# A transformer block on one core: exponents of the weights by DMA, weights split in four pieces, four banks for the down product, block pairs two operands at a time

## Chip, cores and metric

One core of a Trainium2 chip runs the whole block in one launch. The metric is the time of one execution on the device in microseconds (us). TensorE multiplies, VectorE and ScalarE do elementwise work and reductions, GpSimd does elementwise work and can issue DMAs, and SyncE (SP) issues most of the DMAs. Each engine works through its own instructions in the order in which the program was built, and waits on semaphores for the others.

## The reference

```python
x = A_x                                     # 1 x 2048 x 576, float32
n = layernorm(x)
q, k, v = split(n @ wqkv)                   # 32 heads of 18
o = softmax(q @ k.T / sqrt(18)) @ v         # per head
h = x + o @ wo
n2 = layernorm(h)
h2 = h + (gelu_tanh(n2 @ w_gate) * (n2 @ w_up)) @ w_down    # 576 -> 4608 -> 576
```

Everything is float32. The kernel splits each float32 operand into a float16 high part and a float16 low part and adds three float16 products (high by high, high by low, low by high).

## The kernel before

The 2048 rows are four blocks of 512 (`NB = 4`, `TB = 512`). The program has four stages.

1. Layer norm and the products for queries, keys and values.
2. Attention: eight groups of four heads by four row blocks, 32 tiles (`n`), each of 16 steps (`kt`). VectorE finds each row's maximum (L533), TensorE the scores (L530, L577), ScalarE the exponentials (L579), TensorE weighs the values (L583). `out_block` (L591 on) divides by the sums; its denominators are written to DRAM and broadcast back (L613, L614).
3. A transition: during the last three tiles and after them, `wo_block` multiplies by `wo` and adds x, `pair_rows` normalizes rows and builds the operands of the next stage, and the first weights are loaded and split.
4. The feed-forward layer. The 4608 columns are 18 chunks of 256, and two chunks make a super-chunk `sc`. Rows are taken in two halves `p`, each of two blocks of 512.

In stage 4 the two row blocks and the two halves of the contraction are combined in Strassen's manner: seven products instead of eight for each matrix. The left operands are sums and differences of the weight's four blocks (`S1` to `S4`, `A12`, `A22`, `A11`, `A21` in `W8`, built on GpSimd at L787 on), the right ones those of the rows (`B22`, `B11`, `B21`, `T1` to `T4`, built by `pair_rows`). `unit(c, p)` makes both matrices' seven products for chunk c and half p: 14 steps, in each one product of seven matmuls (L868) and the elementwise work that follows it: copies and GELUs on ScalarE, adds and gates on VectorE, then the high and the low part of the result (L879, L882). It ends with an add (L939), a gate (L876), a high and a low part. `down(p)` multiplies both chunks' results by `w_down`: 16 steps, in each a group of twelve matmuls into one bank (L279), which VectorE adds to `nat` (L958).

The weights are prepared by generators that are stepped beside this work. `split_chunk(c)` does the gate matrix and then the up matrix of chunk c: `load_matrix` issues ten DMAs into `W8`; five yields pass; `split_matrix` builds the sums, calls `exponents`, and writes high parts (ScalarE, L796), low parts (VectorE, L800) and a fix of the tail rows (L804), first for operands 4 to 6 and then for 0 to 3. `split_down(sc)` loads 512 rows of `w_down` into `df`, which is the same memory as `W8`, and splits them likewise (L843, L844); its scale depends on both chunks' exponents. `exponents` (L117) takes the largest absolute value of a matrix: VectorE reduces each partition (L125, L128), TensorE transposes the 128 results into a bank (L132), VectorE reduces that row (L134), TensorE multiplies it by ones to bring it to all partitions (L139), and VectorE copies it and shifts out the exponent (L141, L143).

Each `yield` marks a point at which another generator may be stepped; `take(it, n)` steps it n times, `run(it)` steps it to its end. What a step issues stands on each engine's queue behind what was issued before it. One turn of the main loop, from the second super-chunk on, issues:

- `run(nxt[0])`, then `unit(c, 0)` with the preparation beside it (called U1 in the prediction)
- `run(nxt[1])`, then `unit(c + 1, 0)` (U2) with `split_down` beside it
- `run(nxt[2])`, `down(0)` (D1), then `unit(c, 1)` (U3) alone
- `unit(c + 1, 1)` (U4) and `down(1)` (D2), with the preparation of the next super-chunk beside them

`nxt` holds the two `split_chunk` and the `split_down` of the next super-chunk. `beside` takes two steps of the preparation at every other step of the main work and one at the others.

Banks: `unit` uses six of the eight 2 KB banks (`banks`: three for the gate, three for the up matrix; the sixth, u[2], is the first half of the tile `pairs2[1]`). `m_ring` gives banks for the maxima and for `wo_block`; in stage 4 it and `down_ring` are the same ring of two banks, `singles[3]` and the second half of `pairs2[1]`.

`pair_rows(p)` works on four row blocks i of 128 rows: VectorE normalizes two rows' halves, GpSimd builds T1 to T4 (L718 on), then in two pieces (four operands, three operands) VectorE makes high and low parts, and SP issues transposing DMAs (L748) into the operands' place in `X` or `V`. It issues four transposes per i. Half 0 is done beside the last attention tile (n = 31, from kt = 9), half 1 beside `down(0)` of the first super-chunk, in both pieces through the same buffer.

## Time and profile before

| | us |
|---|---|
| median of three runs | 2969.67 (2966.55 to 2971.0) |
| the profiled execution | 2965.44 |
| its span in the profile | 2963.7 |
| TensorE, VectorE, ScalarE, GpSimd busy | 2697.1, 2247.1, 1590.2, 524.8 |

How to read the lines in the prediction. A row of a timeline is: start in us from the start of the span, duration in us, engine, line, operation, output<-inputs, shape, type, count of instructions drawn together; a bracket at its end gives idle time of the engine just before and what ended it. PE is TensorE, DVE is VectorE, ACT is ScalarE, POOL is GpSimd, SPq the issuing of DMAs on SP's queue. A row of the windows is: the window, its length, busy us (and instructions) of PE, PE's weight loads, DVE, ACT and POOL, the granted clock of TensorE, the busy share of the DMA engines and GB/s. A row of the groups has busy us in total, mean ns of one, idle time before them and its releaser. The chain of waits lists what the end of the program waited for, in order of time. Line numbers are those of the kernel before. Names of tiles are those of memory regions: `W`, `WK`, `A`, `V` and `X` are large ones that several uses share.

### The profile page before, as it was taken

Reading aid. Unit: us, or ns where it says so; the run is one execution under the profiler, and the core shown is the slowest. Engines: PE = TensorE matmul, PEld = TensorE weight load, DVE = VectorE, ACT = ScalarE, POOL = GpSimd, SP = SyncE. Lnnn points to the kernel's source line nnn. Section 1 sums busy time; section 2 is a strip of 40 time slices with the busy share of each in tenths; the row PEclk is TensorE's granted clock in tenths of the full one; section 3 lists DMA queues with packets and bytes.
Section 4 is the critical chain, followed back from the end, with each engine's and each line's share of the span. In section 5 each row is a group of like instructions: output and inputs, shape, how many; then the busy total and the mean of one; then the engine's idle time right before and its main releaser. Section 6 shows DMA issues by size and latency. Waiting matters only on the chain.

```text
span 2963.7 us, 43958 instructions
## 1 busy us (share of the span) xinstructions
PE 2697.1 (91%) x16755; PEld 1110.7 (37%) x16755; DVE 2247.1 (76%) x4068; ACT 1590.2 (54%) x1826; POOL 524.8 (18%) x683
## 2 busy tenths in 40 slices
PE   7999999999999999999967699999999999999999
PEld 3542222222222222222323345555555555555555
DVE  6369999999999999999775556565656565656563
ACT  4218888888888888888542133333333333333332
POOL 2102421212121211212140211111111111111100
PEclk9999999999999999999988899999999999999999
DMA  7221010101010100100141211010101010101011
GB/s 211 66 68 49 14 36 13 34 14 38 14 37 14 28 18 19 33 16 23 47 96 40 54 42 36 20 36 20 36 20 36 20 36 20 36 20 37 20 50 41
DMA packets 170855, 111.99 MB, mean 38 GB/s; under 512 B 84596, under 2 KB 151924, under 8 KB 170644
## 3 DMA queue, kind: packets, MB, share of 16 engines
q1 hardware_dynamic: 165284, 99.90, 12.4%
q0 software_dynamic: 5360, 9.29, 1.2%
q8 instruction: 131, 2.15, 0.3%
q14 instruction: 80, 0.66, 0.1%
HBM read 74.45 MB, written 14.42 MB: 30 GB/s over the span
## 4 chain that ended last, share of the span: by engine, by line
DVE 55%; PE 35%; ACT 4%; DMA 3%; issue 2%; SPq 1%; POOL 0%; DVEq 0%; ACTq 0%; POOLq 0%
DVE mx L533 39%; PE pair L279 9%; PE bank L279 9%; PE bank L868 8%; PE pair L868 7%; DVE WK L882 2%; DVE ac_m L125 1%; ACT WK L879 1%; DMA A<-in_B_w_down_dram 1%; DVE nat L958 1%; DVE W L844 1%; DVE tmp L876 1%; DVE W L800 1%; PE bank L583 1%; DMA X<-A 1%
## 5 line engine op out<-in xcount | busy, mean ns | idle before, releaser
L533 DVE TENSOR_REDUCE mx<-bank 128x1 f32<-128x512 f32 x2048 | 1264.6, 682 | 25.4 <-PE bank L530 25.3
L579 ACT ACTIVATE WK<-pair,p_ex_sc 128x1024 f32<-128x1024 f32 x1024 | 1084.5, 1113 | 236.7 <-PE pair L577 235.6
L583 PE MATMUL bank<-WK,V 128*32 128x512 f32 x4096 | 548.3, 607 | 0.1
L279 PEld LDWEIGHTS <-WK 128*128 128x128 f16 x3456 | 338.1, 98 | 156.4 <-issue 51.6
L868 PEld LDWEIGHTS <-W 128*128 128x128 f16 (+1 forms) x2394 | 234.2, 98 | 317.0 <-issue 50.0
L530 PE MATMUL bank<-W 54*128 54x512 f16 x1024 | 289.8, 381 | 38.0 <-DVE mx L533 9.4
L530 PE MATMUL bank<-A 54*128 54x512 f16 x1024 | 279.1, 380 | 35.2 <-DVE mx L533 6.5
L279 PE MATMUL bank<-W,WK 128*128 128x288 f16 x1824 | 253.6, 287 | 29.9 <-DVE nat L958 20.3
L279 PE MATMUL pair<-W,WK 128*128 128x288 f16 x1632 | 226.4, 289 | 21.7 <-DVE nat L958 18.3
L583 PEld LDWEIGHTS bank<-WK,V 128*32 128x32 f32 x4096 | 81.2, 108 | 433.3 <-issue 405.3
L868 PE MATMUL pair<-X,W 128*128 128x512 f16 (+1 forms) x792 | 221.6, 384 | 22.2 <-ACT tmp L889 10.3
L868 PE MATMUL pair<-V,W 128*128 128x512 f16 (+1 forms) x720 | 203.1, 380 | 8.5 <-ACT tmp L918 3.0
L606 POOL TENSOR_TENSOR rp<-rc,minus_one 128x16 f32<-128x16 f32 x28 | 81.8, 2923 | 617.3 <-DMA rc<-nat 617.3
L787 POOL TENSOR_TENSOR A<-A 128x384 f32<-128x384 f32 x36 | 36.3, 1007 | 807.6 <-DVE A L804 407.9
L796 ACT ACTIVATE W<-A,p_s_m 128x1152 f16<-128x1152 f32 (+1 forms) x52 | 72.6, 1412 | 198.2 <-DVE p_s_m L171 198.2
L577 PE MATMUL pair<-W 56*128 56x512 f16 x1024 | 158.7, 378 | 6.0 <-ACT WK L579 5.3
L577 PE MATMUL pair<-A 56*128 56x512 f16 x1024 | 156.1, 376 | 1.5 <-ACT WK L579 0.8
L958 DVE SCALAR_TENSOR_TENSOR nat<-bank,p_dsc,nat 128x288 f32<-128x288 f32 x152 | 78.3, 515 | 97.9 <-PE bank L279 95.8
L530 PEld LDWEIGHTS <-W 54*128 54x128 f16 x1024 | 59.0, 93 | 221.1 <-issue 219.3
L530 PEld LDWEIGHTS <-A 54*128 54x128 f16 x1024 | 56.7, 93 | 208.7 <-issue 205.3
L958 DVE SCALAR_TENSOR_TENSOR nat<-pair,p_dsc,nat 128x288 f32<-128x288 f32 x136 | 70.0, 515 | 81.3 <-PE pair L279 80.0
L868 PEld LDWEIGHTS <-A 128*128 128x128 f16 x882 | 86.2, 98 | 108.2 <-DMA X<-A 5.4
(279 smaller groups left out, 2913.2 us busy)
## 6 DMA issues: line engine op xcount, KB each, us to landing
A<-in_B_w_down_dram SPq DMA_DIRECT2D x9, 1152.0 KB
A<-in_B_w_up_dram SPq DMA_DIRECT2D x72, 128.0 KB
A<-in_B_w_gate_dram SPq DMA_DIRECT2D x68, 128.0 KB
nat<-rc SPq DMA_DIRECT2D x32, 256.0 KB
qk_hi<-qk SPq DMA_DIRECT2D x36, 128.0 KB
qk_lo<-qk SPq DMA_DIRECT2D x36, 128.0 KB
A<-in_A_x_dram SPq DMA_DIRECT2D x32, 144.0 KB
out_dram<-nat SPq DMA_DIRECT2D x16, 288.0 KB
```

Source lines behind the costliest of these rows:

```text
L279: nc.tensor.matmul(dst, a, b, start=(i == 0), stop=(i == len(pairs) - 1))
L530: nc.tensor.matmul(pms[j][:, :TB], Q[r, q0 : q0 + P], K[r, kc * TB : (kc + 1) * TB], start=True, stop=True)
L533: nc.vector.tensor_reduce(mx[:, t, 2 * pr + j, kc : kc + 1], pms[j][:, :TB], axis=AX.X, op=ALU.max)
L577: nc.tensor.matmul(pS[:, j, :TB], K[r, kt * P : (kt + 1) * P], Q[r, qc * TB : (qc + 1) * TB], start=True, stop=True)
L579: nc.scalar.activation(pes[(2 * kt + pr) % NPE], pS[:, :, :TB], AF.Exp, scale=ex_sc)
L583: nc.tensor.matmul(acc[32 * hh : 32 * hh + 32, :TB], Vg[n // NB][:, kt * G4 + hh * VC : kt * G4 + hh * VC + 32], pes[(2 * kt + hh // 2) % ...
L606: nc.gpsimd.tensor_tensor(rc, den, minus_one.to_broadcast([P, R]), op=ALU.pow)
L787: nc.gpsimd.tensor_add(W8[:, S1], W8[:, A21], W8[:, A22])
L796: nc.scalar.activation(wh[:, a:b], W8[:, a:b], AF.Copy, scale=s)
L868: nc.tensor.matmul(bank, w, x_, start=start and i == 0, stop=i == len(mm) - 1, skip_group_check=not start)
L882: nc.vector.tensor_sub(hl[:, 2 * i + j], v, hh[:, 2 * i + j])
L958: nc.vector.scalar_tensor_tensor(nat[:, t, ws], pt[:, :HALF], dsc, nat[:, t, ws], op0=ALU.mult, op1=ALU.add)
```

## The change

- `exponents` no longer uses TensorE: the 128 partial maxima (256 for the down matrix) are written to DRAM, read back into all 128 partitions, and reduced there on VectorE. Four yields lie between the issue of the two DMAs and the reduce.
- `split_matrix` writes its seven operands in four pieces (4 and 5, 6, 0 and 1, 2 and 3) with two yields each, and has a yield with the value "ready" ahead of them; `wait` for a load is 7 yields.
- `load_matrix` broadcasts the tail rows with one DMA per block: eight DMAs in place of ten.
- `down_ring` has four banks of its own: the second half of `pairs2[1]`, `singles[3]`, and two of those that `unit` uses.
- `beside` always takes two steps.
- `pair_rows` works in four pieces of two (the last: one) operands, through three buffers for half 0 and two for half 1; the high part of half 1 is made on ScalarE; it issues six transposes per i. Half 1 follows on `split_down(0)` and so begins in `unit(1, 0)`.
- Chunk 1's gate matrix is loaded and its maximum found during attention's end (`second`, up to "ready"), and the first loads go on GpSimd's queue.
- The tail matmul of `product` takes 128 rows in place of 96.

```diff
     nc.gpsimd.memset(neg, -MSC)
+    am_dram = [dram.tile([2 * P], F32, name=f"am{i}") for i in range(2)]
+    rows_used = []
+
     def exponents(views, name):
         n = len(views)
...
                 yield
         nc.vector.tensor_reduce(am, ac, axis=AX.X, op=ALU.max)
         yield
-        pt = next(m_ring)
-        for i in range(n):
-            nc.tensor.transpose(pt[0:1, i * P : (i + 1) * P], am[:, i : i + 1], id32)
-        a1 = small.tile([1, n], F32, tag=f"a1{n}", name=f"a1_{name}")
-        nc.vector.tensor_reduce(a1, pt[0:1, : n * P].rearrange("o (n p) -> o n p", n=n),
-                                axis=AX.X, op=ALU.max)
-        nc.vector.tensor_scalar_max(a1, a1, 2.0 ** -60)
-        yield
-        pb = next(m_ring)
-        nc.tensor.matmul(pb[:, :n], ones[0:1], a1, start=True, stop=True)
+        row = am_dram[len(rows_used) % 2]
+        rows_used.append(name)
+        bc = view(WK, 22016, (n * P,))
+        nc.sync.dma_start(row[: n * P].rearrange("(p n) -> p n", n=n), am)
+        nc.sync.dma_start(bc, row[: n * P].unsqueeze(0).to_broadcast([P, n * P]))
+        for _ in range(4):
+            yield
         ab = small.tile([P, n], F32, tag=f"ab{n}", name=f"ab_{name}")
-        nc.vector.tensor_copy(ab, pb[:, :n])
+        nc.vector.tensor_reduce(ab, bc.rearrange("q (p n) -> q n p", n=n), axis=AX.X, op=ALU.max)
+        nc.vector.tensor_scalar_max(ab, ab, 2.0 ** -60)
         e = small.tile([P, n], I32, tag=f"e_{name}", name=f"e_{name}")
         nc.vector.tensor_scalar(e, ab.bitcast(I32), 23, None, op0=ALU.logical_shift_right)
         yield
...
             return XT[:, k % 9, o : o + TB]
         return VP[:, p * PIECES + k - 18]
-    def pair_rows(p, region, off, parts_of):
+    def pair_rows(p, region, off, parts, high):
         F7 = view(region, off, (7, HALF))
         B22, B11, B21, T1, T2, T3, T4 = (F7[:, i] for i in range(7))
         F1 = F7.rearrange("p a b -> p (a b)")[:, HALF : HALF + D]
-        for rows in parts_of:
-            nc.gpsimd.memset(rows.rearrange("p (a b) -> p a b", b=5 * P)[:, :, 5 * P - KR :], 0.0)
+        C = 5 * P
+        M2, M3 = 2 * P, 3 * P
+        for rows in parts:
+            nc.gpsimd.memset(rows[:, :, M3 - KR : M3], 0.0)
         for i in range(TPB):
             t1, t2 = 2 * p * TPB + i, (2 * p + 1) * TPB + i
             normed(F1, nat[:, t1], t1)
...
             nc.gpsimd.tensor_sub(T3, B22, b12)
             nc.gpsimd.tensor_sub(T4, B21, T2)
             yield
-            for q, (o0, o1) in enumerate(((0, 4), (4, 7))):
+            for q, (o0, o1) in enumerate(((0, 2), (2, 4), (4, 6), (6, 7))):
                 f = F7[:, o0:o1]
-                rows = parts_of[q]
-                n = o1 - o0
-                r = rows[:, : n * 5 * P].rearrange("p (a b) -> p a b", b=5 * P)
-                M2 = 2 * P
-                nc.vector.tensor_copy(r[:, :, :M2], f[:, :, :M2])
-                nc.vector.tensor_copy(r[:, :, 2 * M2 : 2 * M2 + KR], f[:, :, M2:])
+                rows = parts[q % len(parts)]
+                r = rows[:, : o1 - o0]
+                high(r[:, :, :HALF], f)
                 yield
-                nc.vector.tensor_sub(r[:, :, M2 : 2 * M2], f[:, :, :M2], r[:, :, :M2])
-                nc.vector.tensor_sub(r[:, :, 2 * M2 + KR : 2 * M2 + 2 * KR], f[:, :, M2:],
-                                     r[:, :, 2 * M2 : 2 * M2 + KR])
-                nc.gpsimd.tensor_copy(r[:, :, 2 * M2 + 2 * KR : 2 * M2 + 3 * KR],
-                                      r[:, :, 2 * M2 : 2 * M2 + KR])
+                nc.vector.tensor_sub(r[:, :, M3:], f[:, :, :M2], r[:, :, :M2])
+                nc.vector.tensor_sub(r[:, :, HALF : HALF + KR], f[:, :, M2:], r[:, :, M2:HALF])
+                nc.gpsimd.tensor_copy(r[:, :, HALF + KR : HALF + 2 * KR], r[:, :, M2:HALF])
                 k0, k1 = 5 * o0, 5 * o1
+                flat = rows.rearrange("p a b -> p (a b)")
                 for a, b in ((0, 9), (9, 18), (18, 35)):
                     a, b = max(a, k0), min(b, k1)
                     if a >= b:
...
                     else:
                         v = p * PIECES + a - 18
                         dst = VP[:, v : v + b - a, i * P : (i + 1) * P]
-                    nc.sync.dma_start_transpose(dst, rows[:, (a - k0) * P : (b - k0) * P])
+                    nc.sync.dma_start_transpose(dst, flat[:, (a - k0) * P : (b - k0) * P])
                 yield
...
             for a in range(2):
                 eng.dma_start(W8[:, b + a, :2], main[:, a * P : (a + 1) * P].rearrange(
                     "(c p) f -> p c f", p=P))
-            for r in range(3):
-                eng.dma_start(W8[r * KR : (r + 1) * KR, b : b + 2, 2], tail)
+                eng.dma_start(W8[: 3 * KR, b + a, 2], tail[:, a].unsqueeze(0).to_broadcast(
+                    [3, KR, P]))
     def split_matrix(c, m, hi_on=None):
...
         e = yield from exponents([view(A, W8O + 4 * 4 * KT * P, (2, 2 * KT * P))], f"m{m}")
         nc.vector.tensor_copy(ee[:, m, c % 2 : c % 2 + 1], e)
         s = pow2(e, -1, 266, f"s_m{m}")
-        for a, b in ((4, 7), (0, 4)):
+        yield "ready"
+        for a, b in ((4, 6), (6, 7), (0, 2), (2, 4)):
             if hi_on is None:
                 nc.scalar.activation(wh[:, a:b], W8[:, a:b], AF.Copy, scale=s)
             else:
...
             yield
             nc.vector.scalar_tensor_tensor(wl[:, a:b], W8[:, a:b, :2], s, wh[:, a:b, :2],
                                            op0=ALU.mult, op1=ALU.subtract)
-            yield
             r = slice(2 * KR, 3 * KR)
             nc.vector.scalar_tensor_tensor(wh[r, a:b, 2], W8[r, a:b, 2], s[r], wh[r, a:b, 2],
                                            op0=ALU.mult, op1=ALU.subtract)
...
     scales = [None, None]
-    def split_chunk(c, loaded=False, hi_on=None, wait=5):
+    def until_ready(it):
+        for v in it:
+            yield
+            if v == "ready":
+                return
+
+
+    def split_chunk(c, loaded=False, hi_on=None, wait=7, eng=nc.sync):
         for m, src in enumerate((w_gate, w_up)):
             if m or not loaded:
-                load_matrix(src, c)
+                load_matrix(src, c, eng)
                 for _ in range(wait):
                     yield
             yield from split_matrix(c, m, hi_on)
-    def load_down(sc):
-        nc.sync.dma_start(df, w_down[2 * sc * FC : 2 * (sc + 1) * FC, :].rearrange(
+    def load_down(sc, eng):
+        eng.dma_start(df, w_down[2 * sc * FC : 2 * (sc + 1) * FC, :].rearrange(
             "(c p) n -> p c n", p=P))
-    def split_down(sc, wait=5):
-
-        load_down(sc)
+    def split_down(sc, wait=5, eng=nc.sync):
+
+        load_down(sc, eng)
         for _ in range(wait):
             yield
         ed = yield from exponents([df[:, :2], df[:, 2:]], "dn")
...
         return dsc
     banks = [singles[0], singles[1], singles[2], pairs2[0][:, 0], pairs2[0][:, 1], pairs2[1][:, 0]]
+    down_ring = ring([pairs2[1][:, 1], singles[3], singles[1], pairs2[0][:, 1]])
     tmps = []
     tmp_ring = ring(tmps)
...
             ks = [piece(p, 5 * b + k) for k in range(5)]
             mm = []
             for k in range(2):
-                mm += [(wh[:, a, k], ks[k]), (wh[:, a, k], ks[2 + k]), (wl[:, a, k], ks[k])]
-            mm += [(wh[: 3 * KR, a, 2], ks[4][: 3 * KR])]
+                mm += [(wh[:, a, k], ks[k]), (wh[:, a, k], ks[3 + k]), (wl[:, a, k], ks[k])]
+            mm += [(wh[:, a, 2], ks[2])]
             for i, (w, x_) in enumerate(mm):
                 nc.tensor.matmul(bank, w, x_, start=start and i == 0,
                                  stop=i == len(mm) - 1,
...
             for b in range(1, NB):
                 yield from qk_tile(j, b, next(pair_ring)[:, 0])
+    second = split_chunk(1, eng=nc.gpsimd)
     kept = []
     def keep(it):
...
                 fill = wo_block(qc - 1, m_ring)
                 if qc == 2:
                     fill = chain(fill, pair_rows(0, V, 2 * PIECES * TB + 8960, [
-                        view(V, 2 * PIECES * TB + o, (n * 5 * P,), F16)
-                        for o, n in ((0, 4), (4 * 5 * 2 * P, 3))]))
+                        view(V, 2 * PIECES * TB + 2560 * i, (2, 5 * P), F16) for i in range(3)],
+                        nc.vector.tensor_copy))
             if g == 0 and qc == 0 and kt == NT - 1:
                 run(fill)
                 init_set(sets[1])
...
                 blank_rows()
                 load_matrix(w_gate, 0, nc.gpsimd)
             if n == NS - 2 and kt == NT // 2:
-                side = split_chunk(0, True, nc.vector.tensor_scalar_mul)
+                side = chain(split_chunk(0, True, nc.vector.tensor_scalar_mul, eng=nc.gpsimd),
+                             until_ready(second))
     run(side)
     run(fill)
     weigh(*prev)
...
     next(ob)
     tmps += [small.tile([P, TB], F32, tag="tmp", name="tmp", bufs=3) for _ in range(3)]
     tmps += [view(WK, 19968, (TB,)), view(V, 2 * 2 * PIECES * TB, (TB,)), view(W, 33792, (TB,), F32)]
-    down_ring = m_ring = ring([singles[3], pairs2[1][:, 1]])
+    m_ring = ring([singles[3], pairs2[1][:, 1]])
     it = unit(0, 0)
+    side = second
     take(it, 2)
     take(ob)
     take(it, 3)
     take(ob)
+    take(side, 2)
     take(it, 2)
     fill = wo_block(NB - 1, m_ring)
-    side = split_chunk(1)
     for _ in range(2 * TPB):
         take(fill)
         take(side)
...
         take(side, 2)
     run(side)
-    def beside(main, side, every=2):
-
-        for i, _ in enumerate(main):
-            take(side, 1 + (i % every == 0))
-
-    nxt = [iter(()), iter(()), keep(split_down(0))]
-    side = chain(*nxt)
+    def beside(main, side, n=2):
+
+        for _ in main:
+            take(side, n)
+
+    nxt = [iter(()), iter(()), keep(split_down(0, eng=nc.gpsimd))]
+    side = chain(nxt[2], pair_rows(1, A, MAT, [
+        view(A, MAT + 4 * 7 * HALF + 2560 * i, (2, 5 * P), F16) for i in range(2)], nc.scalar.copy))
     for sc in range(NCH // 2):
         c = 2 * sc
         last = sc == NCH // 2 - 1
...
         beside(unit(c + 1, 0), side)
         run(nxt[2])
         dsc = kept.pop()
-        if sc == 0:
-            side = pair_rows(1, A, MAT, [view(A, MAT + 4 * 7 * HALF, (4 * 5 * P,), F16)] * 2)
         beside(down(0, dsc, last), side)
         run(side)
         if sc == 0:
```

## The prediction

> **What bounds the kernel now.** I read the page's span first, then busy time by window, then TensorE's timeline over one period of the last stage. "Product" is seven matmuls of L868, "group" twelve of L279; one super-chunk (two chunks of 256 columns of the feed-forward layer) is a period.
>
> ```profile
> span 2963.7 us, 43958 instructions
> 220.00:1455.00 1235.00, 1161.20 (x7927) 271.54 (x7925) 1223.43 (x2034) 1050.50 (x1019) 280.78 (x405) 1.00 0.10 25
> 1455.00:1743.00 288.00, 206.25 (x1186) 100.01 (x1185) 164.19 (x354) 88.90 (x108) 66.18 (x80) 0.88 0.28 62
> 1743.00:2963.00 1220.00, 1136.56 (x6574) 640.58 (x6571) 732.79 (x1418) 384.47 (x552) 146.40 (x132) 1.00 0.10 31
> ```
>
> The page is of an execution whose span is 2963.7 us. From 220 to 1455 us VectorE is busy 1223 of 1235 us (attention's row maxima): it is the limit there, and the change puts nothing into that stage before its last tiles. From 1743 on TensorE is busy 1137 of 1220 us at full clock, so what remains are its waits. Between lies a transition of 288 us with TensorE busy only 206 us and a clock of 0.88. One period, by the first product or group of each part (TensorE's timeline; the bracket is idle time before and its releaser):
>
> ```profile
> 1878.45 1.68 PE L868 MATMUL bank<-X,W 128*128 128x512 f16 x7
> 1901.24 1.27 PE L279 MATMUL bank<-W,WK 128*128 128x288 f16 x9
> 1931.78 1.68 PE L868 MATMUL bank<-X,A 128*128 128x512 f16 x7
> 1954.23 1.68 PE L868 MATMUL bank<-X,W 128*128 128x512 f16 x7
> 1980.57 1.63 PE L279 MATMUL bank<-W,WK 128*128 128x288 f16 x12
> 2005.47 1.68 PE L868 MATMUL bank<-X,A 128*128 128x512 f16 x7
> 2026.68 1.68 PE L868 MATMUL bank<-X,W 128*128 128x512 f16 x7
> ...
> 1987.83 1.63 PE L279 MATMUL bank<-W,WK 128*128 128x288 f16 x12
> ```
>
> Six parts: the odd chunk's second half U4 (1878.45 to 1901.24), the down product of that half D2 (to 1931.78), the next even chunk's first half U1 (to 1954.23), the odd chunk's U2 (to 1980.57), D1 (to 2005.47), U3 (to 2026.68). U3 has nothing beside it: 21.21 us, which is 14 products of 1.515 without a wait. The twelve last groups of D1 (1987.83 to 2005.47) follow each other after 1.47 us, so a down product without waits is 16 x 1.47 = 23.52. Against these, U4 loses 1.58, D2 7.02, U1 1.24, U2 5.13, D1 1.38 and U3 nothing: 16.35 of the 148.23 us. What the change can give or take in the steady stage is a change of this sum, eight times (the ninth super-chunk has no next one beside its second half). The waits:
>
> ```profile
> 1888.30 0.27 PE L132 MATMUL bank<-id,am_m 128*1 128x128 f32 x1 [0.59 <-DVE am_m L128]
> 1890.64 1.02 PE L868 MATMUL pair<-X,W 128*128 128x512 f16 x4 [0.25 <-DVE ab_m L141]
> 1902.98 0.42 PE L279 MATMUL bank<-W,WK 128*128 128x288 f16 x2 [0.47 <-ACT WK L879]
> 1904.03 0.30 PE L279 MATMUL bank<-W,WK 128*128 128x288 f16 x1 [0.63 <-DVE WK L882]
> 1907.29 1.63 PE L279 MATMUL bank<-W,WK 128*128 128x288 f16 x12 [1.03 <-DVE nat L958]
> 1961.00 2.74 PE L868 MATMUL pair<-X,W 128*128 128x512 f16 x7 [2.06 <-ACT V L889]
> 1963.53 2.34 PE L868 MATMUL bank<-V,W 128*128 128x512 f16 x7
> 1619.12 0.37 PE L132 MATMUL bank<-id,am_m 128*1 128x128 f32 x1 [8.48 <-DVE am_m L128]
> 1620.55 3.14 PE L868 MATMUL bank<-X,W 128*128 128x512 f16 x7
> ```
>
> Maxima through TensorE cost U4 0.59 and 0.25; D2's first group waits for the unit's last ScalarE and VectorE steps (0.47, 0.63), the third for its bank (1.03, since two banks alternate); in U2 a wait of 2.06 for a ScalarE copy is followed by products of 2.74 and 2.34 where 1.68 is normal, 1.72 more. The last two rows are of the transition: 8.48 us for maxima, then a product of 3.14, 1.46 more than normal.
>
> **The change part by part.** *The maxima.* Per matrix two transposes or one, a matmul and two VectorE operations leave; two DMAs on SP's queue and a VectorE reduce of 128 or 256 elements come. The trace has no such trip. Nearest is the softmax's denominators, written to DRAM and broadcast back:
>
> ```profile
> 1562.74 0.33 SPq L613 DMA_DIRECT2D rc<-rc  x1
> 1564.15 0.59 SPq L614 DMA_DIRECT2D nat<-rc  x1
> ...
> 1564.15 4.50 DMA nat<-rc
> ```
>
> The write's completion releases the next issue 1.41 us after its own. The read costs between the 0.59 of its issue and 4.50 (256 KB; here 64 or 128 KB), so the trip is 2.0 to 5.9; I take 4.2, nearer to the upper row because it is the same kind of broadcast. The old way took 2.3 us, from the transpose at 1888.30 to the product at 1890.64 whose matmul stands behind the copied maximum. The change leaves four yields of cover, and two are taken per step: two steps, 3.0 us. So TensorE loses its short waits in U4 and U1, but VectorE, which executes in order, stands 0 to 2.9 us (1.2 by my value) at the reduce, with the unit's adds and gates queued behind it, and ScalarE's GELUs behind these.
>
> *The pace.* A matrix now has 24 yields (7 wait for the load, 8 in the maxima, 1 "ready", 8 in four pieces); before 16. Two chunk matrices are 48, both chunks 96. Two takes per step give 28 in U4, 32 in D2, 28 in U1: 88. The 8 left are precisely the whole split of the odd chunk's up matrix, which the code then flushes between U1 and U2, as the order of built instructions shows: all VectorE and ScalarE pieces stand behind U1's last ones and ahead of U2's first. Before, at 1.5 per step, 64 yields ended inside U1. U2's second product needs that matrix. VectorE's and ScalarE's rows for the pieces and for U1's end are:
>
> ```profile
> 1957.35 0.69 DVE L939 TENSOR_TENSOR W<-pair,W 128x512 f32<-128x512 f32 x1
> 1959.58 0.69 DVE L882 TENSOR_TENSOR WK<-V,WK 128x512 f16<-128x512 f32 x1 [0.68 <-ACT WK L879]
> ...
> L796 ACT ACTIVATE W<-A,p_s_m 128x1536 f16<-128x1536 f32 x26 | 40.8, 1569 | 0.0
> L796 ACT ACTIVATE W<-A,p_s_m 128x1152 f16<-128x1152 f32 x26 | 32.6, 1255 | 198.2 <-DVE p_s_m L171 198.2
> L800 DVE SCALAR_TENSOR_TENSOR W<-A,p_s_m,W 128x1024 f16<-128x1024 f32 x18 | 23.0, 1280 | 6.9 <-ACT W L796 6.8
> L800 DVE SCALAR_TENSOR_TENSOR W<-A,p_s_m,W 128x768 f16<-128x768 f32 x18 | 18.3, 1015 | 13.2 <-ACT W L796 13.2
> L804 DVE SCALAR_TENSOR_TENSOR W<-A,p_s_m,W 32x512 f16<-32x512 f32 x27 | 20.1, 743 | 0.4
> ```
>
> With T the end of U1's last product: add, gate, high and low take 2.9 us (1957.35 to 1960.27), so VectorE is there at T+3.2; reduce and exponents, six short operations of about 0.2, T+4.3. ScalarE's pieces by the slope of its two rows (0.31 us for 384 elements) are 0.94 and 0.63: T+5.9. VectorE's low parts follow (768 and 1024 elements differ by 0.265, so 0.75 and 0.48, with a tail of 0.5 between): T+7.0. TensorE needs it at T+1.5 and can run two of the product's seven matmuls (0.43) earlier: a stall of 5.1 to 5.8, I take 5.3. The slow clock after it costs at least the 1.46 of one slow product and at most 2.9, two of them; I take 2.0, near the 1.72 of the row at 1961.00.
>
> *U2, the down matrix.* Its load waits until the flushed split has read the same region, about T+10. The rows of the old chain:
>
> ```profile
> 1957.39 0.39 SPq L822 DMA_DIRECT2D A<-in_B_w_down_dram  x1
> 1963.08 1.41 DVE L125 TENSOR_REDUCE ac_dn<-A 128x1 f32<-128x576 f32 x2 [2.21 <-DMA A<-in_B_w_down_dram]
> 1971.61 1.44 ACT L843 ACTIVATE W<-A,p_s_dn 128x576 f16<-128x576 f32 x2 [3.60 <-DVE p_s_dn L171]
> ```
>
> The load takes 5.7, the scale is there 14.2 us after the load's issue (1971.61); with a trip of 4.2 for 2.3 that is 16.1: T+26.1. ScalarE stands at the first scaled copy (it stood 3.60 us already), and the copy that frees bank g0 for the eleventh product is behind it: free at T+27.5, a scaled copy and its own 0.7 later. TensorE arrives at T + 10 x 1.515 + 5.3 + 2.0 = T+22.5 to 24. Stall 3.5 to 5.0, I take 4.4, plus a slow clock of 0 to 2.9 (1.4). U2 then loses 5.3+2.0+4.4+1.4 = 13.1 (10.1 to 16.6).
>
> *Down product on four banks.* The bank waits go: D2's rest 7.02-1.10 = 5.92 becomes 0.3 (0 to 1.0), D1 1.3 (1.0 to 1.5). But the ring's first bank is half of the pair that holds the unit's last product, so the first group now waits for the last add of U4.
>
> ```profile
> 1886.25 1.80 DVE L125 TENSOR_REDUCE ac_m<-A 128x1 f32<-128x768 f32 x2
> ```
>
> VectorE in U4 stands until about 13.7 us after its start (load and block sums 7.8 as at 1886.25, reduces 1.8, trip 4.2), then has 4.6 us of pieces and some 7 x 0.7 of unit operations, and 1 to 2 us of waits on ScalarE: the add is done 4 to 5 us after TensorE's last product. Loss at this boundary 4.6 with a clock loss of 1.4, 6.0 (4.5 to 7.9); before, 1.58 and 1.10. U1 0.2 (0 to 0.5).
>
> Sum after: 6.0+0.3+0.2+13.1+1.3 = 20.9, from 15.6 (4.5+0+0+10.1+1.0) to 27.5 (7.9+1.0+0.5+16.6+1.5). Against 16.35 that is +4.6 (-0.8 to +11.2) a period, +37 us (-6 to +89) for eight.
>
> *Transition.* D1 of the first super-chunk carries the rows of block pairs:
>
> ```profile
> 1648.88 1.27 PE L279 MATMUL bank<-W,WK 128*128 128x288 f16 x9
> 1666.41 3.04 PE L279 MATMUL pair<-W,WK 128*128 128x288 f16 x12 [6.75 <-DVE nat L958]
> 1680.68 3.04 PE L279 MATMUL pair<-W,WK 128*128 128x288 f16 x12 [5.84 <-DVE nat L958]
> 1706.33 3.17 PE L868 MATMUL bank<-X,A 128*128 128x512 f16 x7 [5.09 <-DMA X<-A]
> ...
> 1674.52 2.73 SPq L748 DMA_TRANSPOSE X<-A  x2
> ```
>
> It takes 57.4 instead of 23.5 us, a round of 14.3 for each of four row blocks (1666.41 to 1680.68), because one buffer is filled, transposed and filled again, and VectorE's adds wait in the same queue. After: six transposes per round at 1.37 us of SP (2.73 for two) are a floor of 8.2; 14.3 is the ceiling if two buffers hide nothing; I take 11.5. The rounds begin about 7 us before U2 ends (the down split's 20 yields are ten of U2's 14 steps), and the last transposes land some 3 after: 4 x 11.5 - 7 + 3 = 42, and with TensorE's own rest 45: -12 (-28 to -4). The second chunk loaded during attention takes off part of the 8.48 wait for its maxima: -4 (-8.5 to 0). The first half's eight more transposes (8 x 1.37 = 11 of SP, partly under the row maxima) and the last heads' reciprocal behind a VectorE wait: +4 (0 to 15). The first down matrix's longer chain: +3 (0 to 5). Sum -9 (-36.5 to +16). The gpsimd queue for these loads, the shorter tails' DMAs and the 128-row tail matmul I put at nothing: the loads lie ahead of work that is longer, and a matmul's time goes with its columns; uncovered, one load is the 5.7 above.
>
> Total 2965.4 + 37 - 9 = 2993. (2965.44 is the profiled run's time, 1.7 around its span; the median of the runs is 2969.67, 0.14% above.)
>
> **The rivals.** *Faster: the flush stays hidden.* If VectorE arrives at U1's end without a backlog and the trip is 2.0, so that no reduce blocks, U2 keeps 5.13 and the U4 boundary 2.68: 2.68+0.3+0.2+5.13+1.3 = 9.6, -6.75 x 8 - 9 = -63: 2902. For it: VectorE is busy only 733 of 1220 us. Against: its add at U1's end already comes 3 us late (1957.35). *Only one of U2's two stalls:* the down chain waits anyway while TensorE stalls, so 4.4+1.4 less: 15.1 a period, -10 - 9: 2946. For it: the old chain's 14.2 us passed with a wait of only 2.06. Against: it starts only when the flushed split is done. *Slower still, the clock:* each long stall leaves TensorE slow for two products: the upper sum, +89 - 9 = 3045. For it: 1961.00 and 1963.53 after only 2.06 us idle. The Trainium skill (TensorE: Matmul & The Clock Gate, Part 1: The HAM clock gate) says that the clock halves after an idle window of about 3.4 us and returns after as long a busy one; by that rule, three stalls a period would lose 1.7 us each as an estimate, 5.1 where I take 4.8, and 2995. The row at 1961.00 does not wait for so long an idle time. *The change doesn't do what it says:* the rounds of block pairs stay bound by filling (14.3), and the 12 us are not gained: 3005. For it: SP alone needs 8.2 a round; against: the second buffer.
>
> **How the numbers follow.** Forecast 2993 with 0.42 (its own range 2974 to 3015); hidden flush 0.15; one stall 0.17; clock 0.18; transition not shortened 0.08. Two tenths are left out by 2925 to 3055. 0.2% is 6 us, about what a measurement here can tell from no change. Faster: 0.15 and most of the 0.17, 0.29; same 0.06, from the edges of the forecast and the one-stall case; slower 0.65.
>
> **What would show it.** In the period after: a wait before U2's second product of about 5 us, released by VectorE's or ScalarE's split of the up matrix (right), or none (hidden flush); a wait before its eleventh product, with ScalarE standing for the down scale; D2's first group waiting for L946's add, its other groups without waits; U3 still 21.2 us; rounds of 11 to 12 us in the first D1. The forecast is wrong if the period is under 148 us, or if the transition moves by more than 36.

## The result and the profile after

| | before | after |
|---|---|---|
| median, us | 2970.34 (2966.55 to 2972.71) | 3344.78 (3339.8 to 3355.65) |
| span of the profiled execution, us | 2963.7 | 3353.9 |

The ratio is 1.1267 with a 95% interval of 1.1234 to 1.13: slower by 374 us. The forecast was 2993, 28 above the 2965.4 that it started from, with 3055 as its upper end. The sign was right, the size was not. One of the four executions of a kernel below (four banks alone, the pair's half first) was slow, 4068.51 us at a granted clock of 0.588 where the other three had 0.975 to 0.977, and is left out of its median.

The page of the changed kernel: its span, the chain of waits by engine, and the one group that holds most of the answer (line, engine, operation, tile, shapes, count, busy us and mean ns, idle time before and its releaser).

```profile
span 3353.9 us, 43951 instructions
DVE 45%; PE 28%; DMA 19%; ACT 3%; issue 2%; POOL 1%; SPq 1%; DVEq 0%; ACTq 0%; POOLq 0%
L141 DVE TENSOR_REDUCE ab_m<-WK 128x1 f32<-128x128 f32 x36 | 10.3, 285 | 340.3 <-DMA WK<-am 340.3
```

In the chain, DMA has 19%; in that of the kernel before it had 3%:

```profile
DVE 55%; PE 35%; ACT 4%; DMA 3%; issue 2%; SPq 1%; POOL 0%; DVEq 0%; ACTq 0%; POOLq 0%
```

The new reduce L141 is busy 10.3 us in 36 instructions, and VectorE stood idle ahead of them for 340.3 us until the read of the maxima had landed: 9.7 us in each of 35 waits, where the prediction had 1.2.

One period by parts (windows; the columns are those of the windows before: length, busy us of TensorE, weight loads, VectorE, ScalarE and GpSimd, clock, DMA share, GB/s). In order: U3, U4, D2, U1, U2, D1.

```profile
1928.33:1949.48 21.15, 21.15 (x100) 9.56 (x98) 8.12 (x12) 7.82 (x13) 0.00 (x0) 1.00 0.00 1
1949.48:1986.23 36.75, 23.49 (x99) 10.08 (x98) 19.18 (x36) 11.56 (x19) 4.38 (x4) 0.85 0.12 22
1986.23:2016.80 30.57, 26.45 (x192) 19.99 (x192) 17.21 (x36) 3.71 (x5) 2.94 (x4) 0.90 0.13 27
2016.80:2048.57 31.77, 23.09 (x101) 9.97 (x99) 16.36 (x34) 10.08 (x16) 5.23 (x6) 0.84 0.13 29
2048.57:2095.91 47.34, 28.08 (x99) 10.84 (x98) 24.26 (x53) 15.01 (x24) 0.52 (x1) 0.78 0.16 41
2095.91:2119.43 23.52, 23.52 (x192) 18.78 (x192) 9.12 (x17) 0.62 (x1) 4.28 (x4) 1.00 0.01 3
```

| lost, us | U4 | D2 | U1 | U2 | D1 | sum |
|---|---|---|---|---|---|---|
| before | 1.58 | 7.02 | 1.24 | 5.13 | 1.38 | 16.35 |
| forecast | 6.0 (with D2's first wait) | 0.3 | 0.2 | 13.1 | 1.3 | 20.9 |
| after | 15.5 | 7.1 | 10.6 | 26.1 | 0.0 | 59.3 |

U3, which has nothing beside it, takes 21.15 us as before, and D1 is without a wait. The four parts that have a matrix's maxima beside them lost the time, and their clock is 0.78 to 0.90. This period is 42.9 us longer than the one before (191.10 against 148.23), and it is one of the shorter ones: from the first U3 to the last the eight periods take 1549.2 us against 1186.8, 362 more. The transition adds 28, since the first U3 starts at 1734.15 where it started at 1706.33. Together that is the 390 us between the two profiled spans; the profiled execution is the slowest of the four, 11 us above their median. TensorE's timeline shows where the time went:

```profile
1734.15 3.15 PE L875 MATMUL bank<-X,A 128*128 128x512 f16 x7 [5.43 <-DMA X<-A]
1974.69 3.15 PE L875 MATMUL pair<-V,W 128*128 128x512 f16 x7 [8.42 <-ACT tmp L925]
1986.23 2.98 PE L280 MATMUL pair<-W,WK 128*128 128x288 f16 x12 [4.84 <-DVE V L946]
2006.56 3.04 PE L280 MATMUL bank<-W,WK 128*128 128x288 f16 x12 [4.11 <-DVE nat L965]
2033.20 1.01 PE L875 MATMUL pair<-V,W 128*128 128x512 f16 x2 [8.69 <-DVE WK L903]
2061.56 1.03 PE L875 MATMUL pair<-X,W 128*128 128x512 f16 x2 [11.31 <-ACT W L796]
2087.24 2.42 PE L875 MATMUL bank<-V,W 128*128 128x512 f16 x7 [4.54 <-ACT tmp L921]
```

The first row is the transition's end (the last transposes). None of the other releasers is a DMA: they are VectorE's adds, ScalarE's copies and, at 2061.56, a high part of the split (L796), which stood behind something else. What that was is seen on VectorE (timeline, U1), in the chain of waits and on SP's queue:

```profile
2017.07 0.15 DVE L131 TENSOR_REDUCE am_m<-ac_m 128x1 f32<-128x2 f32 x1
2017.14 0.51 DVE L965 SCALAR_TENSOR_TENSOR nat<-pair,p_dsc,nat 128x288 f32<-128x288 f32 x1
2029.07 0.28 DVE L141 TENSOR_REDUCE ab_m<-WK 128x1 f32<-128x128 f32 x1 [11.43 <-DMA WK<-am]
2032.46 0.69 DVE L903 TENSOR_TENSOR WK<-pair,WK 128x512 f32<-128x512 f32 x1
...
2017.57 7.44 DMA am<-am_m
2025.02 4.02 DMA WK<-am
2076.30 3.32 DMA am<-am_dn
2079.63 3.97 DMA WK<-am
...
2017.09 0.37 SPq L778 DMA_DIRECT2D A<-in_B_w_up_dram  x1
2017.57 0.40 SPq L136 DMA_DIRECT2D am<-am_m  x1
2025.02 0.34 SPq L137 DMA_DIRECT2D WK<-am  x1
```

The partial maxima are ready at 2017.22. The write takes 7.44 us and the read 4.02. VectorE reaches the reduce at 2017.64, 0.1 us after the write is issued, and stands 11.43 us. U1's add L903 comes at 2032.46 and TensorE's next product, which needs its bank, at 2033.20 after 8.69 us. The write of the down matrix's maxima, with two values per partition, takes only 3.32. Over the whole chain 36 writes of one value average 7.5 us, six of two values 3.3, and 43 reads 4.3.

### The profile page after: what moved, and what is told of

Read it like the earlier page. It is cut to its first block, busy times and chain, and to the rows that moved or that the text cites. A ratio compares the mean times of both kernels' runs of the same rounds, so it can differ in the third digit from the quotient of the medians.

```text
span 3353.9 us, 43951 instructions
## 1 busy us (share of the span) xinstructions
PE 2774.7 (83%) x16611; PEld 1132.6 (34%) x16611; DVE 2285.6 (68%) x4187; ACT 1612.0 (48%) x1910; POOL 539.1 (16%) x723
## 4 chain that ended last, share of the span: by engine, by line
DVE 45%; PE 28%; DMA 19%; ACT 3%; issue 2%; POOL 1%; SPq 1%; DVEq 0%; ACTq 0%; POOLq 0%
DVE mx L534 34%; DMA am<-am_m 8%; PE pair L280 8%; PE pair L875 7%; PE bank L280 6%; PE bank L875 6%; DMA WK<-am 5%; DMA A<-in_B_w_down_dram 2%; DVE ac_m L128 1%; DMA am<-am_dn 1%; DMA nat<-rc 1%; DVE A L800 1%; PE bank L531 1%; DVE W L800 1%; DMA A<-in_A_x_dram 1%
## 5 line engine op out<-in xcount | busy, mean ns | idle before, releaser
L875 PEld LDWEIGHTS <-W 128*128 128x128 f16 x2394 | 250.3, 105 | 671.8 <-issue 321.6
L280 PEld LDWEIGHTS <-WK 128*128 128x128 f16 x3456 | 353.8, 102 | 207.1 <-issue 101.0
L875 PE MATMUL pair<-V,W 128*128 128x512 f16 x720 | 238.8, 437 | 166.9 <-ACT tmp L925 47.0
L875 PE MATMUL pair<-X,W 128*128 128x512 f16 x792 | 240.3, 401 | 107.4 <-ACT W L796 102.5
L280 PE MATMUL pair<-W,WK 128*128 128x288 f16 x1728 | 243.7, 299 | 48.7 <-DVE tmp L946 28.6
L280 PE MATMUL bank<-W,WK 128*128 128x288 f16 x1728 | 244.2, 301 | 44.7 <-DVE nat L965 44.7
L141 DVE TENSOR_REDUCE ab_m<-WK 128x1 f32<-128x128 f32 x36 | 10.3, 285 | 340.3 <-DMA WK<-am 340.3
L796 ACT ACTIVATE W<-A,p_s_m 128x768 f16<-128x768 f32 x104 | 83.0, 845 | 313.6 <-DVE p_s_m L172 313.6
L875 PE MATMUL bank<-V,W 128*128 128x512 f16 x414 | 117.7, 417 | 46.5 <-ACT tmp L921 16.9
L875 PE MATMUL bank<-X,W 128*128 128x512 f16 x468 | 136.5, 423 | 0.0
```

What stands on the lines that cost most here:

```text
L280: nc.tensor.matmul(dst, a, b, start=(i == 0), stop=(i == len(pairs) - 1))
L796: nc.scalar.activation(wh[:, a:b], W8[:, a:b], AF.Copy, scale=s)
L875: nc.tensor.matmul(bank, w, x_, start=start and i == 0, stop=i == len(mm) - 1, skip_group_check=not start)
```

## The experiments

All kernels compute the whole reference. Times are medians; the kernel before stood at 2966 to 2969 beside them.

**Maxima by TensorE in the changed kernel**, at the same number of yields. The theory T was that the trip is the cost, F that the flush is, O that other parts are.

```diff
-        nc.sync.dma_start(row[: n * P].rearrange("(p n) -> p n", n=n), am)
-        nc.sync.dma_start(bc, row[: n * P].unsqueeze(0).to_broadcast([P, n * P]))
+        pt = next(m_ring)
+        for i in range(n):
+            nc.tensor.transpose(pt[0:1, i * P : (i + 1) * P], am[:, i : i + 1], id32)
...
         for _ in range(4):
             yield
+        pb = next(m_ring)
+        nc.tensor.matmul(pb[:, :n], ones[0:1], a1, start=True, stop=True)
```

> The changed kernel with its maxima spread by TensorE as before (two bank tiles, transpose, matmul), at the same number of yields, so that the flush between U1 and U2 stays. Theory T (the trip through DRAM, 7.4 us to write and 4.2 to read for each matrix where 4.2 in all was forecast, holds VectorE and nearly everything behind it): the waits at the reduce (340 us over 35) go, the time falls by 330 to 400 us to 2945 to 3015. Rival F (the flush and the pace are the cost): the waits before U2's second product stay near 11 us and the time stays above 3200. Rival O (banks, block pairs, queues of the first loads): above 3250, and the steady period stays near 190 us.

Measured 3046.15, ratio 1.0254 (1.0239 to 1.0269). 299 of the 374 us are gone. U2's second product (TensorE's timeline) waits 2.40 us where it waited 11.31:

```profile
1807.99 1.04 PE L878 MATMUL pair<-X,W 128*128 128x512 f16 x2 [2.40 <-ACT W L799]
```

That refutes F and O as the main cost. The time is 31 us over T's range, so that the rest of the change is dearer than T had it.

**The same with one yield**, so that nothing is flushed: the preparation of both chunks then ends inside U1, and none of its steps are left to be issued in one go ahead of U2.

```diff
-        for _ in range(4):
-            yield
+        yield
```

> As the first, with one yield in place of four ahead of the copied maximum: 21 yields a matrix, 84 for both chunks, within the 88 that U4, D2 and U1 take, so nothing is left to flush. T: the flush is worth the 5 to 7 us that the prediction gave it, 8 periods: 40 to 60 us less than the first kernel, 2895 to 2965. F: far more than 100 us less than the first kernel.

Measured 3029.89, ratio 1.0207 (1.019 to 1.0224): 16 us less. From the first U3 to the last the two traces differ by 24.1 us, 3.0 a period; the rest is that the transition is 6.8 us longer here. So the flush, taken together with the three yields of cover that went with it, costs less than the 40 to 60 expected, and less than the 7.3 a period of the prediction. One period's parts (TensorE's timeline: U3, D2, U1, D1, U3 begin):

```profile
1866.13 1.67 PE L877 MATMUL bank<-X,A 128*128 128x512 f16 x7
1914.29 2.99 PE L282 MATMUL pair<-W,WK 128*128 128x288 f16 x12 [3.65 <-DVE V L948]
1942.69 1.67 PE L877 MATMUL bank<-X,A 128*128 128x512 f16 x7
1998.38 1.63 PE L282 MATMUL pair<-W,WK 128*128 128x288 f16 x12 [0.79 <-DVE tmp L948]
2021.89 1.67 PE L877 MATMUL bank<-X,A 128*128 128x512 f16 x7
```

U3 and U4 take 48.16, 5.7 over their 42.4; D2 28.40, 4.9 over; U1 and U2 55.69, 13.3 over; D1 is clean. The sum is 23.9 against 16.35, 7.5 more in this period. The eight together are 56.4 us longer than before, so nearly all of the 60 us that are left are in the steady stage.

**Eight bytes per partition.** Each maximum is written twice, as the down matrix's two values are.

```diff
+            am2 = small.tile([P, 2], F32, tag="am2", name=f"am2_{name}")
+            nc.vector.tensor_copy(am2, am.to_broadcast([P, 2]))
...
-        nc.sync.dma_start(row[: n * P].rearrange("(p n) -> p n", n=n), am)
+        nc.sync.dma_start(row.rearrange("(p n) -> p n", n=2), am2)
```

> The changed kernel with each partition's maximum written twice, eight bytes for four (as the down matrix has them), and 128 KB read back for 64. Theory S (the write is slow because of its four-byte pieces): the write of a gate or up matrix falls from 7.4 to about 3.3 us as the down matrix has it, and the time by up to 4.1 x 36 = 148 us, 3200 to 3260. Rival Q (the write stands behind the 128 KB load piece that SP issues 0.47 us ahead of it): the write stays at 7 us or more and the time at 3330 to 3350.

Measured 3236.36, ratio 1.0897 (1.0875 to 1.0919), 108 us less than the changed kernel; VectorE's idle time at the reduces of gate and up matrices falls by about as much, from 340.3 to 228.4 us. From this kernel's SP queue and chain of waits, and then SP's queue at the changed kernel's last up matrix, which has no load near it, with two lines of the view of DMA in the window 3210 to 3218 (40 slices of 0.2 us):

```profile
2004.88 0.38 SPq L783 DMA_DIRECT2D A<-in_B_w_gate_dram  x1
2005.31 0.73 SPq L785 DMA_DIRECT2D A<-in_B_w_gate_dram  x1
...
2006.36 3.36 DMA am<-am_m
2009.73 4.30 DMA WK<-am
...
2031.96 3.15 DMA am<-am_dn
```

```profile
3197.49 0.73 SPq L780 DMA_DIRECT2D A<-in_B_w_up_dram  x1
3210.03 0.35 SPq L136 DMA_DIRECT2D am<-am_m  x1
3217.75 0.34 SPq L137 DMA_DIRECT2D WK<-am  x1
...
DMA  0000300000000000000000000000000000000000
DMA packets 144, 0.00 MB, mean 0 GB/s; under 512 B 144, under 2 KB 144, under 8 KB 144
```

The write of a gate or up matrix falls to 3.36, although two pieces of the next load are issued just ahead of it. And in the changed kernel that write takes 7.7 us (3210.03 to 3217.75) with nothing issued on that queue for nearly 12 us before. So the queue is not the reason (Q falls) and the pieces are (S). The packets of that last write have all moved by 3211.1, nearly all in the fifth slice; for the remaining 6.7 us, until SP can issue the read, nothing moves. The time lies between the last packet and the completion. The pieces of a write lie side by side in DRAM, so that their spacing grew with their size: these runs can't tell the two apart.

**The kernel before with the trip alone**, at its own pace and order.

```diff
-        pt = next(m_ring)
-        for i in range(n):
-            nc.tensor.transpose(pt[0:1, i * P : (i + 1) * P], am[:, i : i + 1], id32)
...
-        yield
-        pb = next(m_ring)
-        nc.tensor.matmul(pb[:, :n], ones[0:1], a1, start=True, stop=True)
...
+        nc.sync.dma_start(row[: n * P].rearrange("(p n) -> p n", n=n), am)
+        nc.sync.dma_start(bc, row[: n * P].unsqueeze(0).to_broadcast([P, n * P]))
+        yield
```

> The kernel before with nothing changed but the trip through DRAM in place of TensorE, with its one yield of cover and so with the pace and order of before. T: slower by 250 to 420 us, 3220 to 3390, with VectorE's wait at the reduce near 10 us a matrix. F: within 30 us of before, since no split is flushed. O: within 60 us of before.

Measured 3348.13, ratio 1.1273 (1.1251 to 1.1296). One part of the change brings as much as the whole; with one yield of cover it costs 379, in the changed kernel, with four, 299.

**Four banks alone in the kernel before**, in the order of the change and with the shared pair's half last.

```diff
+    down_ring = ring([pairs2[1][:, 1], singles[3], singles[1], pairs2[0][:, 1]])
...
-    down_ring = m_ring = ring([singles[3], pairs2[1][:, 1]])
+    m_ring = ring([singles[3], pairs2[1][:, 1]])
```

> The kernel before with nothing but the change's ring of four banks for the down product. The prediction's view B: its waits for banks go (1.03 in D2, 1.06 in D1, some of D2's rest), but the first bank is half of the pair whose other half holds the unit's last product, so D2's and D1's first group wait for the last add (about 3 us, and a slow clock of 1.4): D2 7.0 to 5 to 8, D1 1.4 to 1 to 4, within 25 us of before, 2945 to 2995. Rival N (the banks are the gain of the change, the pair costs nothing): 2925 or less. Rival W (the banks are what costs the 60 us that stay when the trip is taken out): 3010 or more.

The second kernel differs in one line:

```diff
-    down_ring = ring([pairs2[1][:, 1], singles[3], singles[1], pairs2[0][:, 1]])
+    down_ring = ring([singles[3], singles[1], pairs2[0][:, 1], pairs2[1][:, 1]])
```

> The same four banks with the shared pair's half last in the ring and not first, so that the first three groups take banks that are free early. B: no group waits for the unit's last add, 10 to 45 us less than the kernel before, 2925 to 2960. N and W: no difference to the order of the change, within 5 us of the run with it.

Measured 2986.07 (ratio 1.0064, 1.0046 to 1.0083) and 2971.48 (1.0014, 1.0004 to 1.0023). From TensorE's timelines, the first in D2 of the first kernel, the second in D2 of the second:

```profile
1912.31 3.04 PE L279 MATMUL pair<-W,WK 128*128 128x288 f16 x12 [3.22 <-DVE V L940]
```

```profile
1917.02 0.27 PE L132 MATMUL bank<-id,am_m 128*1 128x128 f32 x1 [2.22 <-DVE am_m L128]
```

With the pair's half first, D2's first group waits 3.22 us for the unit's last add and then runs slowly (3.04 for 1.63), as the prediction's view had it. With it last that wait is gone, but nothing is gained: TensorE waits 2.22 us for a matrix's maxima instead, just behind the place where it had waited 1.03 for a bank. The bank waits were not what set the end. The first kernel came out within the 25 us of view B; the second, expected 10 to 45 us below the kernel before, is a miss.

**Split in two pieces** in the kernel with maxima by TensorE.

```diff
-        for a, b in ((4, 6), (6, 7), (0, 2), (2, 4)):
+        for a, b in ((4, 7), (0, 4)):
...
+            yield
```

> The changed kernel with maxima through TensorE at one yield, and the split in two pieces as before: 19 yields a matrix, 76 for both chunks. View P (the four pieces take VectorE and ScalarE more instructions in the units and cost the U4 and U2 parts their 4 to 5 us more): 15 to 45 us less than 3030. View V (the pace of two takes a step and the first bank cost them, not the pieces): within 10 us of 3030.

Measured 3063.75, ratio 1.0328 (1.031 to 1.0345): 34 us more, not less. Both views fall. In this kernel the four pieces, with the two more yields that they bring, are a gain at two takes a step.

**The transition alone**: block pairs, early second chunk, gpsimd queue and tail as changed; maxima, pieces, pace and banks as before. The "ready" value is given by the last yield of `exponents`.

```diff
-        yield "ready"
...
-        yield
+        yield "ready"
         return e
```

> The change's block pairs, early second chunk, gpsimd queue and wider tail alone: maxima by TensorE, the split in two pieces, 16 yields, 1.5 takes a step and two banks as before. The prediction gave the transition -9 us (-36 to +16): 2929 to 2985, with rounds of 11 to 12 us in the first D1; view O (these parts are part of the 60 us that stay): 2995 to 3020.

Measured 2961.57, ratio 0.9982 (0.9973 to 0.9992): 4.3 us less than before, where the prediction had 9. It is the only version that is clear of noise below the kernel before, and by 0.2% only. The last row in the first D1 and U3 (TensorE):

```profile
1704.12 3.14 PE L876 MATMUL bank<-X,A 128*128 128x512 f16 x7 [14.87 <-DMA X<-A]
```

The groups of D1 hardly wait for the rounds any more (1.85 us for `nat` at most, where they waited 6.75); U3 does, 14.87 us for the last transposes. It starts at 1704.12, 2.2 us earlier than before. D1 itself is 8.3 us shorter (49.10 against 57.45), but it begins 6.1 us later, at 1655.02.

**Two takes a step alone** in the kernel before, and the transition's kernel with two takes and four pieces.

```diff
-    def beside(main, side, every=2):
-
-        for i, _ in enumerate(main):
-            take(side, 1 + (i % every == 0))
+    def beside(main, side, n=2):
+
+        for _ in main:
+            take(side, n)
```

> The kernel before with two steps of the preparation at every step of the main work and nothing else. Open is what makes up the some 40 us that stay with maxima by TensorE and no flush beyond the 19 us of the first bank. View V (the pace: a load has 2.5 steps of cover, 3.8 us, for 3.3 steps, so VectorE's reduces and TensorE's transposes wait for it): 15 to 60 us slower, 2980 to 3025. View P (the four pieces): within 10 us of before.

> The transition's kernel (2961.6) with the four pieces (18 yields a matrix, 72 for both chunks) at two takes a step. V: the pace costs, 2975 to 3025, as much as the kernel before loses with two takes. P: the pieces cost 15 to 45 us and the pace nothing; then the kernel before with two takes stays near 2966 and this one is at 2980 to 3005. If the pieces help, as the run with two pieces at 3064 says, this one is below what V gives.

Measured 3064.32 (1.0333, 1.0317 to 1.0348) and 3086.29 (1.04, 1.0382 to 1.0418). The pace alone costs the kernel before 97 us, more than the 60 that were sought. One period's parts as above:

```profile
1875.30 1.68 PE L868 MATMUL bank<-X,A 128*128 128x512 f16 x7
1927.31 1.71 PE L279 MATMUL bank<-W,WK 128*128 128x288 f16 x12
1960.50 1.68 PE L868 MATMUL bank<-X,A 128*128 128x512 f16 x7
2012.00 1.63 PE L279 MATMUL bank<-W,WK 128*128 128x288 f16 x12
2036.18 1.68 PE L868 MATMUL bank<-X,A 128*128 128x512 f16 x7
```

U3 and U4 lose 9.6, D2 9.7, U1 and U2 9.1, D1 0.7: 29.0, 12.7 more than before (10.9 on the mean of eight), spread over the parts that have the preparation beside them, and with no flush at all. The second kernel is a miss: it is above the 3025 of view V, and 22 us above the kernel with two takes alone, though it has the four pieces that gained 34 us a moment ago. The prices of the parts don't add up from kernel to kernel; why the pieces don't help here was not found.

**Bank order in the kernel with maxima by TensorE, and four banks in the transition's kernel** (the second order above in both).

> The changed kernel with maxima by TensorE at one yield, and the four banks in the order in which the shared pair's half comes last. View B (the first bank costs here what it cost the kernel before): 10 to 25 us less than 3030, 3005 to 3020. Rival: the first group's wait becomes a wait for maxima or for the unit's last low part, within 8 us of 3030.

> The transition's kernel with the four banks, shared half last: could beat both kernels by more. If the bank waits are hidden behind the maxima, as in the kernel before, 2956 to 2970; if they are on the path with the new transition, 2925 to 2950.

Measured 3042.97 (1.0261, 1.0245 to 1.0276) and 2965.97 (0.9999, 0.9989 to 1.0008). In the first, the order costs 13 us instead of saving 10 to 25, and the rival (within 8 us) misses too: what the first bank's wait costs by itself is not added to what the pace costs. In the second four banks gain nothing again.

**Longer wait for a load at two takes**, in two and in four pieces, on the kernel before.

```diff
-    def split_chunk(c, loaded=False, hi_on=None, wait=5):
+    def split_chunk(c, loaded=False, hi_on=None, wait=7):
```

> The kernel before with two takes a step and seven yields for a load in place of five, that is 3.5 steps of cover where the kernel before has 3.3. View L (two takes cost 97 us because the reduces come ahead of their load's landing, and VectorE stands): most of the 97 us is back, 2960 to 2990. Rival D (two takes cost because the preparation's work then lies denser on VectorE and ScalarE in the same steps, whatever the cover): 3030 to 3070.

> The same with the split in four pieces: 20 yields a matrix. L: as the one with two pieces, within 15 us, 2955 to 2990. D: the pieces spread the dense work and gain what they gained between 3064 and 3030, 25 to 45 us under the one with two pieces.

Measured 3099.78 (1.0442, 1.0424 to 1.0459) and 3078.22 (1.0374, 1.0357 to 1.039). More cover for the loads makes it worse by 35 us, so L falls as a whole; the pieces give 22 back, a little less than the 25 to 45 of D, whose 3030 to 3070 for the first is missed as well. What each part loses in us, the mean of eight periods by TensorE's timelines (over 42.42 for two units and 23.52 for a down product):

| | U3, U4 | D2 | U1, U2 | D1 | sum |
|---|---|---|---|---|---|
| before | 2.0 | 7.0 | 6.2 | 1.3 | 16.5 |
| two takes alone | 8.5 | 9.3 | 8.8 | 0.7 | 27.3 |
| and a longer wait | 2.1 | 12.5 | 16.1 | 0.7 | 31.3 |
| transition, two takes, four pieces | 9.3 | 5.5 | 15.7 | 0.7 | 31.2 |
| changed, maxima by TensorE, one yield | 6.1 | 4.9 | 12.6 | 0.0 | 23.5 |

So L is right for U4, where the longer wait takes the loss away, and wrong for the sum: more is lost in D2 and in U1 and U2. In the view of waits (engine, operation, releaser: us in all, times, longest) TensorE's largest one is the first line with two takes alone, the second with the longer wait:

```profile
PE bank L279 <- DVE nat L958: 47.6, 33, 5.2
PE bank L132 <- DVE am_dn L128: 46.2, 8, 7.2
```

The first is of the down product's groups, which wait for a bank; the second is 5.8 us for each down matrix's maxima, whose own wait of five yields was not lengthened in these kernels. So the pace costs, and where it costs changes with the rest of the kernel; how much of it is the down matrix's short cover and how much the density of the work is not settled.

## Why the prediction missed

*The step that failed* is the price of the trip: "I take 4.2, nearer to the upper row because it is the same kind of broadcast", with 2.0 and 5.9 as its ends. It measured 11.8 for a gate or up matrix (7.5 and 4.3) and 7.6 for the down matrix. The read was inside the bounds (the row had 4.50). The write was not: the row of 1.41 us moves 64 bytes per partition, and the changed kernel's 4. The prediction corrected the read for its size, in kilobytes, and took the write as if it cost nothing more to move less. The kernel with the trip alone shows that this one term is worth 379 us in the kernel before, and the changed kernel without it is 299 us faster. The cover was taken too long as well: 3.0 for two steps of TensorE, where the mean was 2.1 (11.8 less the 9.7 of VectorE's wait) and in U1 0.1, since VectorE had nothing else ahead of the reduce.

*What followed from the term.* The mechanism was put rightly: VectorE, in order, stands at the reduce with the unit's adds and gates behind it. With 11.8 in place of 4.2 it stands 9.7 us in the mean and not 1.2, and each of the five matrices of a period passes it on to TensorE, with a slow product behind it (3.15, 3.04). U1, to which 0.2 was given, lost 10.6 in this way.

*The flush* is in the order, but its price was too high: a stall of 5.3 and 2.0 of slow clock a period, where with fast maxima the stall is 2.40 and removing it gave 3.0. With the slow trip ahead of it the wait is 11.31 (2061.56), since the scale itself is late then. The working sets VectorE free at T+3.2, though in its own rows the add begins only at 1957.35, 3.1 us after U2's first product; in the changed kernel VectorE was free 3.7 us after it (2052.27 against 2048.57), so the slip did no harm.

*The down matrix in U2:* forecast 4.4 at the eleventh product, measured 4.54 (2087.24), but after a U2 that was late by more; it agrees in size, not in working, for the chain was 3.4 us longer and TensorE came later too.

*Four banks:* the wait for the unit's last add is there (4.6; measured 4.84 here, 3.22 alone), but the agreement is partly luck: VectorE leaves U4's reduce 22.6 us after the unit's start (1972.05) and not 13.7, and TensorE was held up too. That the rest of D2 falls to 0.3 is wrong: it is still 7.1, and 4.9 with fast maxima, for the maxima beside D2 take the place of the banks.

*The pace.* The prediction took two takes a step only as a flush. By itself it costs 97 us in a kernel with nothing to flush. This is the second step that failed. That it is most of the 60 us that stay in the changed kernel without the trip and the flush is likely, but not shown: there they are lost in U1 and U2 above all, with two takes alone in U4 (the table above).

*The transition:* -9 forecast, -4.3 us of the whole time measured with fast maxima: D1's 8.3 us of the 12 forecast, and a D1 that begins 6.1 later where +3, +4 and -4 had been put. In the changed kernel the trip makes it +28; with maxima by TensorE at the same yields the first U3 starts at 1701.99. The row blocks' rounds in the first D1 of the changed kernel:

```profile
1703.74 3.83 SPq L747 DMA_TRANSPOSE X<-A  x2
1716.53 3.30 SPq L747 DMA_TRANSPOSE X<-A  x2
1728.74 3.31 SPq L747 DMA_TRANSPOSE X<-A  x2
```

They take 12.8 and 12.2 us, against 11.5 forecast and 14.3 before.

*The clock.* The granted clock is 0.50 in seven stretches of the shown period, each of them at or behind a wait of TensorE. The sum of the windows laid on them (1968.55 to 1978.78, 1985.62 to 1989.02, 2006.10 to 2009.50, 2026.58 to 2036.81, 2053.89 to 2067.53, 2074.37 to 2077.77, 2088.02 to 2091.42):

```profile
sum 47.70, PE 25.94 PEld 10.55 DVE 27.36 ACT 21.19 POOL 0.32; mean PE 3.71 PEld 1.51 DVE 3.91 ACT 3.03 POOL 0.05
```

TensorE is busy 25.9 us at half clock, where a product takes 3.15 us for 1.67, so 13.0 us of the period went to the clock, against 4.8 forecast and 1.7 in the period before (3.40 us at 0.50 from 1961.45). Six of the waits are of over 4 us, where the prediction had three. The Trainium skill (TensorE: Matmul & The Clock Gate, Part 1: The HAM clock gate) says that the clock halves after an idle window of about 3.4 us and returns after a busy one of about that length; as an estimate from these figures, six such waits cost 1.7 us each, 10.2. The trace has somewhat more, and its seventh stretch stands behind a wait of only 2.36 us (2073.30).

## What to carry to other kernels

A small DMA is not cheap for being small: take its price from a row with pieces of the same size (here bytes per partition), not with the same shape of transfer, and where there is none let the upper bound stand far off. Before a wait is moved from one engine to another, ask what is queued behind it there; TensorE's waits for maxima were short, VectorE's held every add and gate of the unit. And a change in the pace at which background work is taken is an edit of its own, to be tried by itself.

## What the hardware showed that was not expected

A write of 128 pieces to DRAM took 7.5 us at 4 bytes each, 3.0 to 3.5 at 8 bytes (means in three kernels, for the down matrix and for the doubled maxima), and 1.41 at 64 bytes: the less was written, the longer it took. Little of that is moving: by the view of DMA the last packet has gone 6.7 us (4 bytes, 3211.1 to 3217.75), 2.3 us (8 bytes, 2077.3 to 2079.63) and 0.4 us (64 bytes, 1563.75 to 1564.15, kernel before) ahead of the next issue. The Trainium skill (DMA: Bandwidth & Descriptors, Specifications) says that below 512 bytes the DMA engines do read-modify-write. No run here shows that, and the rule does not tell 4 bytes from 64, where the time goes by five. Why 4 cost twice as much as 8, size or spacing, was not tried.

A wait of one length does not always slow the clock. In the kernel before TensorE waits 2.04 or 2.06 us for the same copy of U2 in each of eight periods; behind three of these waits the granted clock is 0.50 for 3.40 us (windows from 1961.45, 2258.41 and 2702.14), behind the other five it stays 1.00. The prediction's row of 2.74 us at 1961.00 is one of the three.
